# Pooled attention and a two-layer block: a second level of the seven-product scheme in the last two units of the first layer, with copies and sums moved to GpSimd

## The chip, the cores and the metric

The kernel runs on one core of one Trainium2 chip. The metric is device time in microseconds (us) of a whole execution; lower is better. In the profile the engines are called PE (TensorE, with PEld for its weight loads), DVE (VectorE), ACT (ScalarE), POOL (GpSimd) and SP (SyncE, which issues most of the DMAs).

## The reference, cut to what matters

All data are fp32: 8 batches, 8 heads, 576 positions, head size 64.

```python
k_p, v_p = mean of k and of v over groups of 8 positions      # 72 keys
attn = softmax(q @ k_p.T / 8) @ v_p                           # per batch and head
x = attn as (4608 tokens, 512)
h = x @ w_in                                                  # w_in: 512 x 2048
g = h + sin(alpha * h) ** 2 / (alpha + 1e-9)                  # alpha: per column of h
out = g @ w_out                                               # w_out: 2048 x 512
```

## The kernel before

**Both layers by seven products.** Each layer is a product of matrices cut in 2 x 2 blocks, done with seven block products in place of eight (the scheme of Strassen and Winograd). The price are sums of blocks on both sides: sums of w_in (`self.A[1..7]`), of x (`self.bt`, by `sums_of_x`, L817), and sums of the products afterwards. In the output layer the scheme is applied twice, one level inside the other, 49 block products for 64; the sums of w_out for that are made once (`load_w_out`, L725, and `inner_w`, L743).

**First layer.** `hidden(u, extra)` handles a unit of 512 tokens; there are nine units, 0 to 8. A unit has four groups J = 0 to 3, and a group has seven slots k = 0 to 6, so 28 slots, slot = 7 J + k. In a slot PE does one product p of the group, in the order 1, 5, 6, 2, 7, 3, 4. A product is four matmuls with 128 weights rows and columns and 256 tokens (L849). The profile holds two records for each such fp32 matmul. The products accumulate in four PSUM banks b1, b5, b6, b7 of a group; ACT copies one bank into the next where the scheme wants a product in two sums (L823) and makes the sine (L1009) and its square (L1016); DVE makes the sums h (L822) and g (L1061: one form with a PSUM input, 512 wide, and one with two SBUF inputs, 1024 wide). Then g goes to DRAM (`store_g`).

In the order of a unit, product 4 of group J waits until DVE has read the bank b7 in the L822 of slot 5 of that group. Where J = 1 the second half of product 4 may be put into slot 7.

**Second level in units 1 to 6.** Three of the 28 products of these units are done by seven small products in turn: product 5 in groups J = 2 and 3 (called i5), product 1 in J = 3 (i1). Such a product is seven matmuls of 128 tokens (L1039) in place of four of 256. `inner_product` cuts it into steps that `hidden` places between other products:

- a: products 1 and 5 into a spare bank y; ACT copies the first into half of the bank (L1043), the second into a small tile `m5` (L1045)
- b: products 6 and 2; ACT copies a quarter of the bank (L1049)
- d: product 7; DVE adds `m5` (L1054)
- e: products 3 and 4, which accumulate on what DVE wrote

The sums of w_in that these products need are made once, in unit 0 (`inner_w_in`), the sums of x in each unit (`inner_x`); both by `sums` on POOL (L807). In units 1 to 6 POOL also pools k and v (L132) and scales the softmax (L375), for the attention of the next batch that runs beside the first layer. i1 of the next group begins in slot 5 of the group before.

**The last two units.** There is no attention left to compute in units 7 and 8, and all their products are of the first level. `run` puts work for the output layer into their slots: in unit 7 w_out is loaded (`load_w_out`, four DMAs of 1 MB on SP into tiles `raw`), and a generator is advanced by `next(w)` in chosen slots: ACT copies the raw blocks into place (L716, 16 copies of 128 x 512), DVE makes the outer sums (L725, 16) and in unit 8 the inner sums of five of the seven weights (L743, four each; a sixth, p = 5, in slots 23 to 27; the seventh in the output layer). In slots 22, 25 and 27 of unit 8 the output layer starts (`outputs`): in slot 22 DVE makes four sums of 128 x 768 (L1303), in slots 25 and 27 PE does the first output products (L1364).

Each engine runs its own instructions in the order in which the program lists them, and waits in front of an instruction for what it needs; the slots are that order, written out by hand.

Of the kernel before, what the change touches and what calls it, by code (L numbers as in the profile page):

```python
# [40 lines left out]
class Kernel:  # L41
# [650 lines left out]
    def load_w_out(self, wp):  # L692
# [18 lines left out]
        def put(i, k):  # L711

            for j, t in enumerate(((b11, b12), (b21, b22))[i]):
                yield
                for n in range(2):
                    nc.scalar.copy(out=t[:, k:k + 4, n * P:(n + 1) * P].rearrange("p k (a c) -> p k a c", a=4),  # L716
                                   in_=raw[i, k][:, :, j, :, n, :])
        yield from put(0, 0)
        yield from put(1, 0)
        for c in range(0, kk, 2):  # L720
            if c == 2:
                yield from put(0, 4)
            yield
            s = slice(c, c + 2)
            tt = lambda o, x, y: nc.vector.tensor_tensor(out=o[:, s], in0=x[:, s], in1=y[:, s], op=OP.subtract)  # L725
            tt(t1, b12, b11)
            tt(t2, b22, t1)
            tt(b12, b22, b12)

            tt(t4, b21, t2)  # L730
            if c == 2:
                yield from put(1, 4)
        for p in (1, 2, 4, 6, 7):
            yield
            self.inner_w(p, wp)
        yield

    def inner_w(self, p, wp):

        nc = self.nc  # L740
        x = self.wb[p]
        b = lambda i, j: x[:, :, i - 1, j - 1, :].rearrange("p (k j) d -> p k j d", k=2)
        tt = lambda o, x, y: nc.vector.tensor_tensor(out=o, in0=x, in1=y, op=OP.subtract)  # L743
# [12 lines left out]
        return steps  # L756
# [24 lines left out]

    def inner_w_in(self):

        w = self.q_tile(0)[:]
        at = 0
        for p, J0 in ((5, 2), (1, 3)):
            n = self.NJ - J0
            A = self.A[p][:].rearrange("p k (J j m) -> p k J j m", j=2, m=P)[:, :, J0:]
            L = lambda i, j: A[:, j, :, i]
            s1, s2, s3, s4 = (w[:, at + i * n * P:at + (i + 1) * n * P].rearrange("p (J m) -> p J m", m=P) for i in range(4))  # L790
            at += 4 * n * P
# [3 lines left out]
    def inner_x(self, u):  # L795

        for p, x, out in ((5, self.bt[u][:, 0], self.last[:, 0:4 * P]),
                          (1, self.xT[u][:, 0:2, 0:TH], self.ex[:, 5].rearrange("p h x -> p (h x)")[:, 0:4 * P])):
            R = lambda i, j: x[:, i, j * P:(j + 1) * P]
            t1, t2, t3, t4 = (out[:, i * P:(i + 1) * P] for i in range(4))  # L800
            self.sums(((t1, R(0, 1), R(0, 0), OP.subtract), (t2, R(1, 1), t1, OP.subtract), (t3, R(1, 1), R(0, 1), OP.subtract), (t4, R(1, 0), t2, OP.subtract)))
            self.X2[p] = {1: R(0, 0), 2: R(1, 0), 3: R(1, 1), 4: t4, 5: t1, 6: t2, 7: t3}

    def sums(self, steps):
# [14 lines left out]
    def hidden(self, u, extra):  # L819
# [4 lines left out]
        sin, square, early = self.sin, self.square, lambda G: G.J == (0 if G.u else 1)  # L824
        two = 0 < u < self.B - 1
        split = lambda J: u == 0 and J == 2
        end = lambda J: u == 0 and J == 3

        def begin(J):
# [4 lines left out]
                                p5=None, i1=None, i5=None, early=J == (0 if u else 1))  # L834
            if two and J > 1:
                G.i5 = self.inner_product(G, 5, b5, 7)
            if two and J == 3:
                G.i1 = self.inner_product(G, 1, b1, 6)
# [21 lines left out]
        for slot in range(7 * self.NJ):  # L860
# [61 lines left out]
            elif k == 3:  # L922
                late = J == 0 and two
# [3 lines left out]
                if G.i1:  # L927
                    square(Q, 1, 1)
                    squares(Q, 0)
# [18 lines left out]
            elif k == 4:  # L948
                if G.i1:
                    copy(G.b7[:], G.b6[:])  # L950
# [16 lines left out]
            elif k == 5:  # L967
# [5 lines left out]
                N = None  # L973
                if two and J + 1 == 3:
                    N = self.next = begin(J + 1)
# [5 lines left out]
            else:  # L981
                if J == 0 and two and Q:
                    self.store_g(Q)
# [4 lines left out]
                if not N:  # L988
                    last()
                    extras()  # L990
                    product(G, 4, G.b7, part=(0, 1))
                    if not (two and J == 1):
                        product(G, 4, G.b7, part=(2, 3))
# [33 lines left out]
    def inner_product(self, G, p, ps, y):  # L1027
# [13 lines left out]
        def a():  # L1041
            products((1, 5), (y[:, 0], y[:, 1]), True)
            nc.scalar.copy(out=f[:, 0], in_=y[:, 0:1].to_broadcast([P, 2, P]))  # L1043
            m5[p] = self.sm.tile([P, 1, P], F32, name=f"m{p}", bufs=1)
            nc.scalar.copy(out=m5[p][:], in_=y[:, 1:2])  # L1045

# [4 lines left out]
        def d():  # L1051
            products((7,), (c[2],))
            x = ps.rearrange("p i t -> p (i t)")[:, P:3 * P].rearrange("p (i t) -> p i t", i=2)
            nc.vector.tensor_tensor(out=f[:, :, 1], in0=x, in1=m5[p][:].to_broadcast([P, 2, P]), op=OP.add)  # L1054

# [127 lines left out]
    def carry(self, u):  # L1183
# [6 lines left out]
        if u == 0:  # L1190
# [39 lines left out]
            at(9, self.load_q, 2)  # L1230
            at(23, self.inner_w_in)
            for e in range(2):
# [336 lines left out]
    def run(self):  # L1569
        nc, tc = self.nc, self.tc  # L1570
        pool = lambda s, n, b, **kw: s.enter_context(tc.tile_pool(name=n, bufs=b, **kw))
        with ExitStack() as top:
# [9 lines left out]
            with ExitStack() as one:  # L1582
# [35 lines left out]
                self.W2, self.X2 = {}, {}  # L1618
                self.R = {}
                self.first_batch()  # L1620
                self.s = self.hp.tile([P, 2, JW, 2, TH], F32, name="s", bufs=1)
                for u in range(self.NU):
                    x = self.carry(u)
                    if u == self.B - 1:
# [4 lines left out]
                        next(w)  # L1629
                        for i in (9, 10, 12, 13, 15, 16, 17, 18, 20, 21, 23):  # L1630
                            x[i].append(lambda: next(w))
                    elif u > self.B - 1:
                        homes.close()
                        homes = rest_homes
                        self.gq = pool(top, "gq", 1, side="right")
                        for i in (6, 10, 13, 14, 17, 20):
                            x[i].append(lambda: next(w))
                        x[5].append(lambda: self.load_g(0, ("r11", "r12")))
                        for i, f in zip((23, 25, 25, 27), self.inner_w(5, None)):
                            x[i].append(f)  # L1640
                        o = self.outputs()
# [48 lines left out]
```

## Time and profile before

| | |
|---|---|
| median of 3 runs | 900.12 us (899.48 to 900.14) |
| the profiled execution | 900.87 us, span 899.1 us |
| PE busy | 893.3 us, 99% of the span |
| DVE, ACT, POOL busy | 674.5, 440.9, 211.8 us |
| granted TensorE clock | 1.000 |
| unit 5, J = 2 to its slot 25 | 332.98 to 352.46 us |
| units 7 and 8 | about 416 to 515.7 us |
| POOL after 405 us | idle |

The span runs from the first to the last instruction of one execution under the profiler; its own time is 1.8 us longer, and the median of the runs is 0.75 us below that. Times in the views of the trace are us from the span's start; in a line of the timeline the first number is the start, the second how long the group of instructions lasts, and `x2` how many there are. A line of the chain has start, length, engine, tile written and line. In the groups of instructions, the numbers after the bar are the busy us in all and the mean ns of one.

### The profile page before, as it was taken

The page shows a single profiled execution, that of the slowest core. Times are in us where ns is not written, and L with a number is a line of the kernel's source. Part 1 is how long each engine was busy: PE and PEld are TensorE (multiplying, and loading weights), DVE is VectorE, ACT ScalarE, POOL GpSimd, SP SyncE. Part 2 cuts the span into 40 slices and gives each one's busy share as a digit, 9 for nine tenths or more (in the row PEclk, how much of TensorE's full clock was granted, in tenths as well). Part 3 has the DMA queues.
Part 4 walks back from the last instruction along what each step waited for, and adds up shares of the span by engine and source line. Part 5 has one row for each costly group of instructions (what it writes and reads, how often), then busy time and mean ns, then how long its engine had stood idle before and what let it go on. Part 6 is the DMA issues. An engine that isn't in the chain of part 4 may idle for free.

```text
span 899.1 us, 16074 instructions
## 1 busy us (share of the span) xinstructions
PE 893.3 (99%) x6226; PEld 814.7 (91%) x6226; DVE 674.5 (75%) x910; ACT 440.9 (49%) x1017; POOL 211.8 (24%) x217
## 2 busy tenths in 40 slices
PE   9999999999999999999999999999999999999998
PEld 5787888888888888888888999999999999999998
DVE  6786766768577685764557889898887896996885
ACT  5696776877768778687976621111121211111111
POOL 5798552824428253430000000000000000000000
PEclk9999999999999999999999999999999999999999
DMA  9946957759587595648216253716435345164002
GB/s 259 252 153 201 240 149 204 195 156 256 144 209 191 172 242 138 182 126 313 80 65 233 95 186 91 243 36 211 124 88 162 102 150 164 38 185 149 19 19 53
DMA packets 119531, 141.01 MB, mean 157 GB/s; under 512 B 45776, under 2 KB 86496, under 8 KB 119456
## 3 DMA queue, kind: packets, MB, share of 16 engines
q1 hardware_dynamic: 116288, 137.39, 52.8%
q10 hardware_dynamic: 3168, 2.61, 1.0%
q8 instruction: 49, 0.80, 0.4%
q14 instruction: 26, 0.21, 0.1%
HBM read 75.37 MB, written 47.19 MB: 136 GB/s over the span
## 4 chain that ended last, share of the span: by engine, by line
PE 98%; DMA 1%; POOL 0%; DVE 0%; issue 0%; ACTq 0%; ACT 0%; POOLq 0%
PE PS L849 46%; PE PS L1364 43%; PE PS L1039 3%; PE PS L318 2%; PE PS L613 2%; PE PS L626 1%; DMA p<-in_v_dram 1%; DMA q<-in_q_dram 0%; PE PS L571 0%; PE PS L290 0%; PE PS L279 0%; PE PS L479 0%; PE PS L569 0%; POOL tr L451 0%; PE PS L487 0%; POOL p L184 0%
## 5 line engine op out<-in xcount | busy, mean ns | idle before, releaser
L849 PE MATMUL PS<-home,a 128*128 128x256 f32 x1104 | 258.1, 381 | 0.1
L849 PEld LDWEIGHTS PS<-home,a 128*128 128x128 f32 x1104 | 205.3, 190 | 32.4 <-issue 4.5
L849 PE MATMUL PS<-home,as 128*128 128x256 f32 x768 | 182.7, 381 | 0.0
L849 PEld LDWEIGHTS PS<-home,as 128*128 128x128 f32 x768 | 141.7, 190 | 19.9 <-ACT PS L823 1.2
L1364 PE MATMUL PS<-s,wb 128*128 128x192 f32 x672 | 116.2, 326 | 0.0
L1016 ACT ACTIVATE s<-s,c 128x256 f32<-128x256 f32 (+1 forms) x228 | 113.5, 564 | 0.0
L1364 PEld LDWEIGHTS PS<-s,wb 128*128 128x128 f32 x672 | 110.4, 190 | 0.1
L822 DVE TENSOR_TENSOR h<-PS,p 128x512 f32<-128x512 f32 x72 | 49.3, 684 | 62.3 <-PE PS L849 36.9
L132 POOL TENSOR_TENSOR kvin<-kvin 96x768 f32<-96x768 f32 (+3 forms) x42 | 74.0, 1762 | 70.6 <-DMA kvin<-in_v_dram 69.0
L1009 ACT ACTIVATE s<-h,al 128x256 f32<-128x256 f32 x144 | 65.6, 509 | 38.5 <-DVE h L822 35.0
L1535 ACT COPY PS<-PS 128x192 f32<-128x192 f32 x42 | 12.7, 303 | 145.2 <-PE PS L1364 133.4
L1364 PE MATMUL PS<-r,wb 128*128 128x192 f32 x432 | 79.0, 326 | 0.0
L1364 PEld LDWEIGHTS PS<-r,wb 128*128 128x128 f32 x432 | 71.7, 190 | 0.1
L1364 PE MATMUL PS<-s,a 128*128 128x192 f32 x384 | 70.2, 326 | 0.0
L1009 ACT ACTIVATE s<-PS,al 128x256 f32<-128x256 f32 x144 | 60.1, 470 | 19.1 <-PE PS L849 18.1
L1061 DVE TENSOR_TENSOR h<-PS,s 128x512 f32<-128x512 f32 x36 | 24.8, 688 | 56.6 <-ACT s L1016 56.6
L1364 PEld LDWEIGHTS PS<-s,a 128*128 128x128 f32 x384 | 63.7, 190 | 0.0
L823 ACT COPY PS<-PS 128x512 f32<-128x512 f32 x72 | 41.4, 576 | 34.9 <-PE PS L849 30.1
L1061 DVE TENSOR_TENSOR h<-h,s 128x1024 f32<-128x1024 f32 x36 | 57.1, 1586 | 1.1 <-ACT s L1016 0.9
L1564 ACT COPY PS<-PS 128x192 f32<-128x192 f32 x42 | 12.7, 303 | 89.8 <-PE PS L1364 89.8
L1303 DVE TENSOR_TENSOR s<-r 128x768 f32<-128x768 f32 x54 | 51.4, 952 | 5.1 <-PE PS L1364 2.8
L1364 PE MATMUL PS<-s,we 128*128 128x192 f32 x288 | 52.7, 326 | 0.0
(218 smaller groups left out, 1316.7 us busy)
## 6 DMA issues: line engine op xcount, KB each, us to landing
g_bridge<-h SPq DMA_DIRECT2D x72, 512.0 KB
r<-g_bridge SPq DMA_DIRECT2D x15, 1536.0 KB
x<-g_bridge SPq DMA_DIRECT2D x8, 1536.0 KB
out_dram<-o SPq DMA_DIRECT2D x90, 96.0 KB
kvin<-in_k_dram SPq DMA_DIRECT2D x14, 576.0 KB
q<-in_q_dram SPq DMA_DIRECT2D x7, 1024.0 KB
kvin<-in_v_dram SPq DMA_DIRECT2D x14, 512.0 KB
aM<-tr SPq DMA_DIRECT2D x54, 92.0 KB
```

The lines of the kernel that those rows point to most:

```text
L132: self.nc.gpsimd.tensor_tensor(out=t[..., 0:w] if w > D else out, in0=t[..., 0:w], in1=t[..., w:2 * w], op=OP.add)
L318: nc.tensor.matmul(ps[e][r0 + r:r0 + r + q.shape[-1], h, :], q[s], kb[s, hp, :], start=True, stop=True)
L613: nc.tensor.matmul(o[r:r + 64], w, x, start=start and i < 2, stop=False, skip_group_check=True)
L822: add = lambda o, x, y: nc.vector.tensor_tensor(out=o, in0=x, in1=y, op=OP.add)
L823: copy = lambda o, x: nc.scalar.copy(out=o, in_=x)
L849: nc.tensor.matmul(ps[:, jj, :], self.A[p][:, kk, f * P:(f + 1) * P], x[:, kk, :], start=(start and n == 0), stop=(kk == 1), skip_group_ch ...
L1009: self.nc.scalar.activation(out=G.s[:, i, jj, j, :], in_=src[:, jj], func=AF.Sin, scale=self.al[:, f:f + 1])
L1016: self.nc.scalar.activation(out=x, in_=x, func=AF.Square, scale=self.c[:, f:f + 1])
L1039: nc.tensor.matmul(o, W[m][:, G.J - J0], X[m], start=start and n == 0, stop=True, skip_group_check=True)
L1061: add = lambda o, x, y: self.nc.vector.tensor_tensor(out=o, in0=x, in1=y, op=OP.add)
L1303: tt = lambda o, x, y, op: nc.vector.tensor_tensor(out=o, in0=x, in1=y, op=op)
L1364: nc.tensor.matmul(out, W[:, J // 2, J % 2, :], A[:, J, :], start=(start and J == 0), stop=(J == self.NJ - 1), skip_group_check=True)
```

## The change

- Units 7 and 8 take the second level for five products each: i5 in J = 1, 2, 3 and i1 in J = 2, 3. In units 1 to 6 nothing is changed (`busy` marks them, in place of `two`).
- The sums of w_in and x for that get homes of their own. In unit 7 (`homes_in_seven`): a free x tile and the two tiles `we1`, `we2` of w_out's inner sums. In unit 8 (`homes_in_eight`): tiles of the output layer's sums (`s30`, `s01`, `s20`) for x and for i5 of J = 1, and, from slot 8 on, the J = 0 slices of A[4], A[5], A[6], A[7] for the rest. All on POOL, in slots 0, 2 and 8.
- The 16 copies of w_out's raw blocks go from ACT to POOL, in two steps (slots 2 and 4 of unit 7) that stand in POOL's queue behind the sums for i5 and i1. DVE's 16 outer sums are now one to a step, in slots 15 to 25 of unit 7 and 1 and 2 of unit 8.
- The inner sums of w_out for p = 1, 2, 6, 7, 5 go from DVE to POOL (four instructions of 512 each); p = 4 stays on DVE in slot 9 of unit 8. In POOL's queue of unit 8 the order is: sums for i5 and i1 (8 of 128, then 4 of 128, then 8 of 256), weights p = 1, 2, 6, 7, 5.
- In the groups with i1 of units 7 and 8 the copy of b6 into b7 is made in slot 3 and not in slot 4.

Counted in the built programs, PE has 40 matmuls of 256 columns less and 70 of 128 columns more, POOL 72 instructions more. In unit 8, group J = 3, DVE's queue has the L822 of the group before, the L1054 of i1, the last L822, then the four L1303 of slot 22, then the L1054 of i5 (slot 23).

```diff
         def put(i, k):
             for j, t in enumerate(((b11, b12), (b21, b22))[i]):
+                for n in range(2):
+                    nc.gpsimd.tensor_copy(out=t[:, k:k + 4, n * P:(n + 1) * P].rearrange("p k (a c) -> p k a c", a=4),
+                                   in_=raw[i, k][:, :, j, :, n, :])
...
+        for k in (0, 4):
+            yield
+            put(0, k)
+            put(1, k)
+        for c in range(0, kk, 2):
+            s = slice(c, c + 2)
+            for o, x, y in ((t1, b12, b11), (t2, b22, t1), (b12, b22, b12), (t4, b21, t2)):
+                yield
+                nc.vector.tensor_tensor(out=o[:, s], in0=x[:, s], in1=y[:, s], op=OP.subtract)
-        for p in (1, 2, 4, 6, 7):
+        for p in (1, 4, 2, 6, 7, 5):
             yield
-            self.inner_w(p, wp)
+            self.inner_w(p, wp, None if p == 4 else nc.gpsimd)
...
+    def homes_in_seven(self, wo, x):
+        X = self.home(0, [P, 2048])
+        self.set_homes(X[:, 0:512], X[:, 512:1024], X[:, 1024:1152], X[:, 1152:1280])
+        we = [wo.tile([P, 3, 2, 2, P], F32, name=n)[:].rearrange("p a b c d -> p (a b c d)") for n in ('we2', 'we1')]
...
+        x[0].append(lambda: self.inner_x(7, (5,)))
+        x[0].append(lambda: self.inner_w_in(((5, 1, 4),), homes[:4]))
+        x[0].append(lambda: self.inner_x(7, (1,)))
+        x[0].append(lambda: self.inner_w_in(((1, 2, 4),), homes[4:]))
...
+    def homes_in_eight(self, x):
+        a, b = (self.gq.tile([P, self.NJ, self.T], F32, name=n)[:].rearrange("p J c -> p (J c)") for n in ("s30", "s01"))
+        self.set_homes(b[:, 0:512], a[:, 0:512], b[:, 512:640], b[:, 640:768])
+        used = [self.A[p][:, k, 0:JW * P] for p in (4, 5, 6, 7) for k in range(2)]
+        c = self.gq.tile([P, self.NJ, self.T], F32, name="s20")[:].rearrange("p J c -> p (J c)")
+        x[0].append(lambda: self.inner_x(8, (5,)))
+        x[0].append(lambda: self.inner_w_in(((5, 1, 2),), [c[:, i * P:i * P + P] for i in range(4)]))
+        x[2].append(lambda: self.inner_x(8, (1,)))
+        x[8].append(lambda: self.inner_w_in(((5, 2, 4), (1, 2, 4)), used))
...
-        two = 0 < u < self.B - 1
+        busy = 0 < u < self.B - 1
+        I5, I1 = ((2, 3), (3,)) if busy else {7: ((1, 2, 3), (2, 3)), 8: ((1, 2, 3), (2, 3))}.get(u, ((), ()))
...
-                        for i in (9, 10, 12, 13, 15, 16, 17, 18, 20, 21, 23):
+                        self.homes_in_seven(wo, x)
+                        for i in (2, 4, 15, 15, 16, 16, 17, 17, 18, 22, 22, 23, 23, 24, 24, 25):
                             x[i].append(lambda: next(w))
...
-                        for i in (6, 10, 13, 14, 17, 20):
+                        self.homes_in_eight(x)
+                        for i in (1, 2, 9, 9, 10, 27, 27, 27):
                             x[i].append(lambda: next(w))
                         x[5].append(lambda: self.load_g(0, ("r11", "r12")))
-                        for i, f in zip((23, 25, 25, 27), self.inner_w(5, None)):
-                            x[i].append(f)
```

More of the change, by code (lines that the diff above doesn't have):

```diff
@@ L713, in put, with inner_w @@
             for j, t in enumerate(((b11, b12), (b21, b22))[i]):
-                yield
[L715 to L722, printed above, removed]
-            yield
[L724 to L732, printed above, removed]
-        for p in (1, 2, 4, 6, 7):
-            yield
-            self.inner_w(p, wp)
+                for n in range(2):
[8 more added lines that the diff above has]
+            for o, x, y in ((t1, b12, b11), (t2, b22, t1), (b12, b22, b12), (t4, b21, t2)):
+                yield
+                nc.vector.tensor_tensor(out=o[:, s], in0=x[:, s], in1=y[:, s], op=OP.subtract)
+        for p in (1, 4, 2, 6, 7, 5):
+            yield
+            self.inner_w(p, wp, None if p == 4 else nc.gpsimd)
         yield
-    def inner_w(self, p, wp):
+    def inner_w(self, p, wp, eng=None):
         nc = self.nc
@@ L780, in abank, with inner_w_in @@
         return self.psum(shape, 5 + self.aturn)
[L782 to L788, printed above, removed]
+    def inner_w_in(self, groups, homes):
+        homes = iter(homes)
+        for p, J0, J1 in groups:
+            n = J1 - J0
+            A = self.A[p][:].rearrange("p k (J j m) -> p k J j m", j=2, m=P)[:, :, J0:J1]
@@ L922, in hidden @@
             elif k == 3:
-                late = J == 0 and two
+                late = J == 0 and busy
                 if Q and not late and not G.i5 and not split(J):
@@ L927, in hidden @@
                 if G.i1:
+                    if not busy:
+                        copy(G.b7[:], G.b6[:])
                     square(Q, 1, 1)
@@ L948, in hidden @@
             elif k == 4:
-                if G.i1:
+                if G.i1 and busy:
                     copy(G.b7[:], G.b6[:])
@@ L973, in hidden @@
                 N = None
-                if two and J + 1 == 3:
+                if J + 1 in I1:
                     N = self.next = begin(J + 1)
@@ L981, in hidden @@
             else:
-                if J == 0 and two and Q:
+                if J == 0 and busy and Q:
                     self.store_g(Q)
@@ L991, in hidden @@
                     product(G, 4, G.b7, part=(0, 1))
-                    if not (two and J == 1):
+                    if J + 1 not in I5 or J + 1 in I1:
                         product(G, 4, G.b7, part=(2, 3))
```

37 lines of the change are left out of this document (24 added, 13 removed).

## The prediction

> **What bounds the kernel now.** I read the chain that ended last first, from the page and then in order of time around the last three units of the first layer.
>
> ```profile
> PE 98%; DMA 1%; POOL 0%; DVE 0%; issue 0%; ACTq 0%; ACT 0%; POOLq 0%
> ```
>
> ```profile
> 332.98 0.44 PE PS L1039 x4
> ...
> 352.46 2.33 PE PS L613 x40
> ...
> 410.99 96.89 PE PS L849 x448
> 507.88 1.30 PE PS L1364 x8
> ```
>
> The second column is us. From 410.99 PE runs 448 records (224 matmuls, two records each) of the first layer in 96.89 us: 0.4325 us for one of 256 columns, 1.730 for a product of four, and not one gap. So PE's own time sets the end, a saved PE us is a won us, and a new PE wait is a lost one. The first two lines price the form that the change spreads: from 332.98 to 352.46, 19.48 us, unit 5 runs three second-level products (21 matmuls of 128 columns) among 34 of 256 columns. 34 × 0.4325 = 14.70, so 21 take 4.78: 0.2275 each, small waits included; four records without waits take 0.44, 0.22 each.
>
> Next, the timeline of the vector engines, because the change gives GpSimd (POOL) 72 instructions where it has had none.
>
> ```profile
> 67.27 1.26 POOL L688 TENSOR_TENSOR a<-a,a 128x512 f32<-128x512 f32 x1
> 67.51 2.11 DVE L1061 TENSOR_TENSOR h<-h,s 128x1024 f32<-128x1024 f32 x1
> 68.50 2.25 POOL L688 TENSOR_TENSOR as<-a,as 128x512 f32<-128x512 f32 x1
> ```
>
> A DVE instruction with two SBUF inputs, 1.21 when alone (507.22 in the same view), took 2.11: it ended 1.09 after the POOL instruction did. The POOL instruction behind it ended 1.13 after DVE, for 1.27 alone. They take turns whole. DVE instructions with a PSUM input are not touched: L822 and L1054 last 0.68 and 0.43 with POOL busy or idle. How a run of them alternates is seen at the start of unit 6:
>
> ```profile
> 362.96 0.94 DVE L817 TENSOR_TENSOR home<-home 128x512 f32<-128x512 f32 x1
> 363.43 0.78 POOL L807 TENSOR_TENSOR last<-home,last 128x128 f32<-128x128 f32 x1
> 363.82 0.94 DVE L817 TENSOR_TENSOR home<-home,home 128x512 f32<-128x512 f32 x1
> 364.18 0.90 POOL L807 TENSOR_TENSOR last<-home 128x128 f32<-128x128 f32 x1
> ```
>
> **What the change is worth on PE.** Ten products of 1.730 us go (17.30). Seventy matmuls of 128 columns come: 70 × 0.2275 = 15.9, or 15.4 at 0.22 without waits. Gain 1.4 us at the pace of units 1 to 6, 1.9 at best. I take 1.4, because the same hand-overs (PE, ACT copy, PE, DVE sum, PE) come with it. What follows is whether PE meets a new wait.
>
> **ACT.** 16 copies (L716, 0.6 each) leave unit 7; each second-level product adds 0.36 + 0.28 + 0.25 (L1043, L1045, L1049). In group J=2, which now runs both kinds and leads to another such group, I stacked ACT's queue from starts of unit 5 (0.40 or 0.36 per sine, 0.40 per square, 0.48 per copy of 512): it reaches the next L1043 7.3 us after i5.b starts, and PE asks for that copy at 7.7. Nothing lost; without this cover some tenths.
>
> **POOL's times.** Two inputs of 512 take 1.27 (L688 below), with the wait on the one before about 1.29; of 256, 0.73; of 128, 0.45. No row shows a copy. From below, a memset, which only writes, costs 0.85 ns per element (1071 less 422 over 768), 0.53 us for 512; from above, the sum's 1.27. I take 0.65, near the memset, since one stream in and one out is nearer to it than two in.
>
> ```profile
> L688 POOL TENSOR_TENSOR a<-a,a 128x512 f32<-128x512 f32 x4 | 5.1, 1272 | 0.0
> L807 POOL TENSOR_TENSOR q<-as 128x256 f32<-128x256 f32 x2 | 1.5, 728 | 0.0
> L1114 POOL MEMSET tr<- 128x1152 f32 x1 | 1.1, 1071 | 0.0
> L1601 POOL MEMSET ex<- 128x384 f32 x1 | 0.4, 422 | 0.0
> ```
>
> The Trainium skill, "GPSIMD Engine Reference", § 3.1, gives about 1.03 cycles per element at 1.2 GHz to bodies of up to two operations, an estimate of 0.44 us for 512 before dispatch; by it the copies would end some 2 us sooner, and the sum would be the same.
>
> **Unit 7.** It starts at 416.2; x sums for p5 run 417.2 to 420.3 (as in unit 6, against L817), weights for p5 (4 × 1.0) with one L1061 in between to 425.6, x and weights for p1 to 430.4. PE wants the first at slot 7, 427.5, and needs only what was ready by 421.5; it wants p1's at 436.8. Then 16 copies: 430.4 + 10.4 + 1.2 for one L1061 = 442. DVE's first L725 (slot 15) comes at 441 and needs only the first four. So they are nearly past each other: nothing lost. The w_out loads keep their place on SP; DMA moves their 4 MB by 427, before the copies. Cover: the spread slots 15 to 25. L1061 in J=1 waits for a copy at most, and unit 5 shows that such a wait (2.41 at 341.65, L822 behind it done at 344.67) still let PE start product 4 at 344.83.
>
> **Unit 8.** It starts at 463.9 (464.6 less 0.7). x sums and the first weights are done by 472; slot 7 is at 475.2. The sums in slot 8 wait for the J=0 slices of A[4], read last at 475.2 + 0.44 + 1.73 + 0.87 = 478.2. From there POOL never rests: 8 × 0.73, then inner_w of 1, 2, 6 and 7, 16 × 1.29, and two L1061 that hold it 1.2 each: 478.2 + 5.8 + 20.6 + 2.4 = 507, and inner_w(5) is still to come. J=2's own sums are there in time: the fifth (for i1.a, slot 12 at 484.5) at 482.
>
> Now J=3. Call T the start of its i5.b: 475.2 + 14.8 + 11.75 = 501.7. In DVE's queue the four L1303 of slot 22 (first sums of the output layer, two SBUF inputs) stand ahead of the L1054 of i5.d. In the kernel before they took 3.7 us and nobody waited:
>
> ```profile
> 503.02 0.95 DVE L1303 TENSOR_TENSOR s<-r 128x768 f32<-128x768 f32 x1
> 504.01 0.96 DVE L1303 TENSOR_TENSOR s<-s,r 128x768 f32<-128x768 f32 x1
> 504.88 0.95 DVE L1303 TENSOR_TENSOR s<-r 128x768 f32<-128x768 f32 x1
> 505.75 0.95 DVE L1303 TENSOR_TENSOR s<-r,s 128x768 f32<-128x768 f32 x1
> ```
>
> In unit 5, where T is 347.68, DVE is free at T − 1.0 and PE starts i5.e, which needs that L1054, at T + 4.17:
>
> ```profile
> 346.03 0.68 DVE L822 TENSOR_TENSOR h<-PS,s 128x512 f32<-128x512 f32 x1
> ...
> 347.68 0.39 PE L1039 MATMUL PS<-last,q 128*128 128x128 f32 x2
> ...
> 351.85 0.39 PE L1039 MATMUL PS<-home,q 128*128 128x128 f32 x2
> ```
>
> Without POOL the four end at T + 2.7 and L1054 at T + 3.2: covered by 1.0 us. With POOL saturated they take turns: −1.0, a first wait of 0.55 (0 to 1.13), 0.95 + 3 × 0.82 of DVE (0.95 less the 0.13 that a waiting instruction saves), 3 × 1.13 of POOL: T + 6.35, L1054 done at T + 6.8. PE waits 2.6 us (2.1 to 3.2). Behind i5.e stand the first output matmuls, products 7, 3 and 4; PE has no gap later in which to make this up, so all of it reaches the end.
>
> **Other parts.** 20 sums (L743) leave DVE for POOL, ten L1054 come: DVE is lighter and not the bound. The last POOL sum delays one L1303 of slot 27 by up to 1.1 us; its product comes 5 us later. inner_w(5) is ready by about 513; it is used 45 us into the output layer. Nothing for either.
>
> **Sum.** −1.4 + 2.6 = +1.2 us. The profiled execution took 900.87, 899.1 of it span; it should become 902.1 (span 900.3). The median of the runs, 900.12, lies 0.75 below it, so I predict 901.3, about +0.13%. A measurement of this kernel tells some 0.2% (1.8 us) from no change.
>
> **Rivals.**
> Hidden (0.22): the turns do not cost what I say, and the gain shows. For it: once two DVE instructions went past a waiting POOL one undisturbed (31.30 and 31.90, 0.67 and 0.68, POOL 2.09 for 0.59). If DVE passes in pairs, one turn of 1.13 is left and the wait is 0.3 or less. Against it: six unit starts show strict turns. 900.12 − 1.4 = 898.7; at the best pace 898.2, just over 0.2% (0.07 of the 0.22). The Trainium skill, "SBUF — State Buffer", § Who interferes with whom, lets whichever starts first keep the shared ports for its whole instruction; by that rule and the rows at 67.27 I keep this rival small.
>
> Slow copies (0.12): a POOL copy costs what a sum does. Then 16 × 1.29 reach past 451, and in J=2 of unit 7 eight two-input DVE instructions (seven L725, one L1061) each wait a turn of 1.13 before the L822 that product 4 waits for: 9 us, less the time that DVE idles there and 0.9 of slack, about 4.3 at PE. 901.3 + 4.3 = 905.6. It decides from some 1.0 us a copy on. Against it: the memset's slope.
>
> Small waits (0.08): hand-overs in four groups with both kinds, without the attention's matmuls between them, lose 0.3 us each: 902.5.
>
> **Numbers.** My case has 0.58; its wait of 2.1 to 3.2 and gain of 1.4 to 1.9 give 900.3 to 902.3, with the tail of the DVE queue behind unknown; I put 0.22 of it above 901.9. Slower: 0.22 + 0.12 + 0.08 = 0.42. Faster: 0.07. Same: 0.36 + 0.15 = 0.51. The range from 898.5 to 903.6 leaves out most of the slow copies and the best pace.
>
> **Right or wrong.** Right: in unit 8, J=3, the four L1303 last about 2 us each with POOL instructions between them, PE stands 2 to 3 us before i5.e, waiting for L1054, and nowhere else in units 7 and 8 for more than some tenths. Wrong: L1303 at 0.95 (hidden), POOL copies above 1.0 with waits at product 4 in J=2 of unit 7 (slow copies), waits for ACT at i1.b (small waits), or POOL idle before 500.

## The result and the profile after

The changed kernel is slower by about half a per cent: a median of 904.35 us (five runs, 903.14 to 905.12) against 899.48 us (five runs of the kernel before, 898.73 to 900.14); the ratio of the times is 1.0048, 95% interval 1.0036 to 1.0060 (the medians alone would give 1.0054). The profiled execution took 905.12 us, 903.3 of it span. The prediction said 901.3, 898.5 to 903.6: the sign is right, the size is far too small.

In what follows line numbers are those of the changed kernel: L873 is the matmul of 256 columns (L849 before), L1065 that of 128 (L1039), L1390 the output layer's (L1364), L1080 the sum into PSUM that i5.e waits for (L1054), L845 the sums h (L822), L1087 the sums g (L1061), L1329 the output layer's sums (L1303), L736 the inner sums of w_out (L743), L715 the copies (L716). In kernels with lines added the numbers move by one to three.

The chain that ended last, as in the first fence of before: PE's share has gone from 98% to 41%, because the chain now leaves PE and runs back through a load.

```profile
PE 41%; DVE 1%; DMA 1%; issue 0%; SPq 0%; DVEq 0%
```

The timeline of PE where unit 8 ends. The number in brackets is the idle time ahead of the line, with what ended it: PE finishes product 2 of the last group and waits for L1080.

```profile
504.68 1.89 PE L873 MATMUL PS<-home,a 128*128 128x256 f32 x8
509.42 0.49 PE L1065 MATMUL PS<-home,as 128*128 128x128 f32 x2 [2.85 <-DVE PS L1080]
```

The timelines of DVE and POOL at the same place show why L1080 is late. Before, the four sums of slot 22 lasted 0.95 each. Now each takes its turn with a POOL sum, and the L1080 of i5 stands behind all four:

```profile
501.19 2.01 DVE L1329 TENSOR_TENSOR s<-r 128x768 f32<-128x768 f32 x1
503.23 1.91 DVE L1329 TENSOR_TENSOR s<-s,r 128x768 f32<-128x768 f32 x1
505.07 2.02 DVE L1329 TENSOR_TENSOR s<-r 128x768 f32<-128x768 f32 x1
507.01 2.01 DVE L1329 TENSOR_TENSOR s<-r,s 128x768 f32<-128x768 f32 x1
508.95 0.42 DVE L1080 TENSOR_TENSOR PS<-PS,s 128x256 f32<-128x256 f32 x1
...
502.46 1.87 POOL L736 TENSOR_TENSOR a<-wb,a 128x512 f32<-128x512 f32 x1
504.30 1.98 POOL L736 TENSOR_TENSOR wb<-wb 128x512 f32<-128x512 f32 x1
506.23 1.98 POOL L736 TENSOR_TENSOR as<-wb,a 128x512 f32<-128x512 f32 x1
```

So far this is what the prediction described. The table of stretches shows what it did not have. Its columns are the stretch, its length, busy us and instructions of PE, PEld, DVE, ACT and POOL, then the granted TensorE clock, DMA share and GB/s:

```profile
507.00:509.00 2.00, 0.00 (x0) 0.00 (x0) 2.00 (x3) 0.64 (x2) 2.00 (x2) 1.00 0.00 0
509.00:510.60 1.60, 1.18 (x8) 1.18 (x9) 1.60 (x4) 0.43 (x1) 1.52 (x2) 1.00 0.00 0
510.60:512.00 1.40, 1.40 (x7) 1.40 (x6) 0.64 (x1) 0.89 (x3) 1.40 (x1) 0.50 0.00 0
512.00:514.00 2.00, 2.00 (x6) 1.56 (x5) 0.00 (x0) 1.28 (x3) 1.59 (x2) 0.50 0.94 351
514.00:516.00 2.00, 2.00 (x11) 1.74 (x10) 0.69 (x1) 0.34 (x1) 0.00 (x0) 0.99 0.47 173
```

From 510.6 to 514.0 the clock is 0.5. PE is busy all that time and does half as much: records of 256 columns start 0.43 us apart instead of 0.216. The drop begins 1.2 us after PE has started again, so PE is not idle in it, and a table of busy times alone would not show it. It costs 3.4 / 2 = 1.7 us.

The chain in order of time then passes through the load that the output layer waits for. The last piece is the first matmul of a product that began at 535.00 without a wait before; it now waits 0.2 us:

```profile
519.74 8.38 DMA r<-g_bridge
...
535.75 3.37 DVE x L1329
...
539.16 5.96 PE PS L1390 x35
```

POOL itself does what was forecast. The groups of its copies: the first eight (`wb<-wb`) last 0.61 us each; in the mean of the second eight (`wb<-r`) one that waited for DVE is included.

```profile
L715 POOL COPY wb<-r 128x512 f32<-128x512 f32 x8 | 5.5, 736 | 0.0
L715 POOL COPY wb<-wb 128x512 f32<-128x512 f32 x8 | 4.5, 613 | 0.0
```

### The profile page after: what moved, and what is told of

The parts are those of the page before. It is cut to its first block, busy times and chain, and to the rows that moved or that the text cites. A ratio compares the mean times of both kernels' runs of the same rounds, so it can differ in the third digit from the quotient of the medians.

```text
span 903.3 us, 16343 instructions
## 1 busy us (share of the span) xinstructions
PE 893.0 (99%) x6286; PEld 815.4 (90%) x6286; DVE 671.3 (74%) x900; ACT 440.5 (49%) x1039; POOL 277.4 (31%) x289
## 5 line engine op out<-in xcount | busy, mean ns | idle before, releaser
L873 PE MATMUL PS<-home,a 128*128 128x256 f32 x1072 | 254.7, 382 | 0.1
L873 PEld LDWEIGHTS PS<-home,a 128*128 128x128 f32 x1072 | 198.9, 191 | 30.9 <-issue 4.6
L873 PE MATMUL PS<-home,as 128*128 128x256 f32 x720 | 174.2, 382 | 0.0
L873 PEld LDWEIGHTS PS<-home,as 128*128 128x128 f32 x720 | 131.1, 190 | 17.9 <-ACT PS L846 1.6
L1390 PE MATMUL PS<-s,wb 128*128 128x192 f32 x672 | 116.2, 326 | 0.0
L1042 ACT ACTIVATE s<-s,c 128x256 f32<-128x256 f32 (+1 forms) x236 | 115.5, 556 | 0.0
L1390 PEld LDWEIGHTS PS<-s,wb 128*128 128x128 f32 x672 | 110.4, 190 | 0.1
L845 DVE TENSOR_TENSOR h<-PS,p 128x512 f32<-128x512 f32 x72 | 49.2, 683 | 63.3 <-PE PS L873 40.1
L1390 PE MATMUL PS<-r,wb 128*128 128x192 f32 x432 | 79.7, 328 | 0.0
L1390 PEld LDWEIGHTS PS<-r,wb 128*128 128x128 f32 x432 | 72.1, 191 | 0.0
L1390 PE MATMUL PS<-s,a 128*128 128x192 f32 x384 | 70.2, 326 | 0.0
L1390 PEld LDWEIGHTS PS<-s,a 128*128 128x128 f32 x384 | 63.7, 190 | 0.0
L1087 DVE TENSOR_TENSOR h<-PS,s 128x512 f32<-128x512 f32 x36 | 24.7, 686 | 46.9 <-ACT s L1042 46.9
L1329 DVE TENSOR_TENSOR s<-r 128x768 f32<-128x768 f32 x54 | 53.6, 992 | 5.5 <-PE PS L1390 2.8
L1087 DVE TENSOR_TENSOR h<-h,s 128x1024 f32<-128x1024 f32 x36 | 55.3, 1537 | 2.5 <-ACT s L1042 2.3
L1390 PE MATMUL PS<-s,we 128*128 128x192 f32 x288 | 52.7, 326 | 0.0
```

The source lines that it names most:

```text
L845: add = lambda o, x, y: nc.vector.tensor_tensor(out=o, in0=x, in1=y, op=OP.add)
L873: nc.tensor.matmul(ps[:, jj, :], self.A[p][:, kk, f * P:(f + 1) * P], x[:, kk, :], start=(start and n == 0), stop=(kk == 1), skip_group_ch ...
L1042: self.nc.scalar.activation(out=x, in_=x, func=AF.Square, scale=self.c[:, f:f + 1])
L1087: add = lambda o, x, y: self.nc.vector.tensor_tensor(out=o, in0=x, in1=y, op=OP.add)
L1329: tt = lambda o, x, y, op: nc.vector.tensor_tensor(out=o, in0=x, in1=y, op=op)
L1390: nc.tensor.matmul(out, W[:, J // 2, J % 2, :], A[:, J, :], start=(start and J == 0), stop=(J == self.NJ - 1), skip_group_check=True)
```

## A measure that leaves the start out

Profiled executions do not reach one and the same instruction of the first layer at the same time: the 321st record of PE starts at 33.84 us in before, at 34.05 in after, and between 32.05 and 33.62 in the ten kernels below, all with the same instructions up to there. That is 2 us of scatter ahead of this record, while the first loads come in, and more than the change was to be worth; what makes it was not tested. So beside the times I compare one stage: from PE's 3201st record (in unit 6, the same instruction in all kernels) to its 2000th record from the end (in the output layer, also the same). From that one to the last record it is 324.84 us in every kernel.

| kernel | stage, us | against before | ratio of the times (95%) |
|---|---|---|---|
| before | 189.98 | | |
| after | 194.14 | +4.16 | 1.0048 (1.0036 to 1.0060) |
| e1_hold | 189.19 | −0.79 | 0.9994 (0.9985 to 1.0003) |
| e2_busy | 193.47 | +3.49 | 1.0029 (1.0020 to 1.0038) |
| e3_three | 190.26 | +0.28 | 1.0007 (0.9998 to 1.0016) |
| e5_pool_alone | 190.00 | +0.02 | 1.0003 (0.9994 to 1.0011) |
| e6_spaced | 189.75 | −0.23 | 0.9989 (0.9980 to 0.9998) |
| e7_five | 197.18 | +7.20 | 1.0072 (1.0056 to 1.0087) |
| e8_six | 193.36 | +3.38 | 1.0036 (1.0022 to 1.0049) |
| e9_pool_spaced | 190.01 | +0.03 | 0.9999 (0.9990 to 1.0007) |
| e10_twice | 189.38 | −0.60 | 0.9992 (0.9983 to 1.0001) |
| e11_three | 193.83 | +3.85 | 1.0051 (1.0036 to 1.0065) |

The stage is of one execution each, the ratio of four to eleven runs. The stages of e2, e7 and e8 contain 1.1 us that PE waits in unit 7 and that has nothing to do with their edits (see e6). Where two kernels differ by less than 0.1%, the intervals do not tell them apart.

## Experiments

Theory: the change wins about 1.5 us on PE, and loses it to one wait, at i5.e of the last group of unit 8, which POOL's inner sums make by taking turns with DVE; the wait costs its own length and after that a stretch at half clock. Rivals: the new products themselves or POOL's copies lose the time, with the wait an accident beside it; or the clock falls for another reason than PE's idle time.

**e1_hold: take away what POOL does during the four sums.** One small POOL sum reads the result of the fourth L1329, and POOL's sums for p = 7 and 5 stand behind it; those for p = 6 move from slot 27 to slot 20, ahead of it.

```diff
+        nc.gpsimd.tensor_tensor(out=self.held[:], in0=A[0, 0][3][:, 0, 0:64], in1=A[0, 0][3][:, 0, 64:128], op=OP.add)
...
-                        for i in (1, 2, 9, 9, 10, 27, 27, 27):
+                        for i in (1, 2, 9, 9, 10, 20, 27, 27):
```

> GpSimd's eight sums for p = 7 and 5 stand behind a small GpSimd sum that reads the result of the last of the four L1329 of slot 22; nothing else is changed against the changed kernel. Turns theory (the L1329 take turns with GpSimd, the L1080 behind them comes late, PE idles, and the idle costs a stretch at half clock): the four L1329 last 0.95 us each, PE does not wait before i5.e of J = 3 in unit 8, the granted clock stays at 1.0, and the time falls by 3.0 + 1.7 us from the changed kernel, to 1.0 to 1.5 us under the kernel before (ratio 0.9985). Hand-over theory (the second level itself makes PE wait in these units, GpSimd or not): L1080 is still late, the wait of about 3 us stays, ratio 1.004 to 1.005.

Measured: 899.23 us against 899.61, ratio 0.9994 (0.9985 to 1.0003). The timelines of DVE, POOL and PE:

```profile
500.18 0.95 DVE L1329 TENSOR_TENSOR s<-r 128x768 f32<-128x768 f32 x1
...
502.91 0.95 DVE L1329 TENSOR_TENSOR s<-r,s 128x768 f32<-128x768 f32 x1
503.78 0.42 DVE L1080 TENSOR_TENSOR PS<-PS,s 128x256 f32<-128x256 f32 x1
...
503.94 0.32 POOL L1514 TENSOR_TENSOR held<-s 128x64 f32<-128x64 f32 x1 [3.79 <-DVE s L1329]
...
505.40 0.38 PE L1065 MATMUL PS<-home,as 128*128 128x128 f32 x2
```

With POOL held for 3.79 us the four sums take 0.95 again, L1080 is ready 1.2 us before PE wants it, no wait stands ahead of i5.e and the clock is 1.0 after it. The time fell short of what was expected: 0.9994 in place of 0.9985, and the stage is 0.79 us under before where 1.0 to 1.5 were expected; most of what is missing is in the gain, below. Setting the two kernels' PE records side by side, after lies 1.02 us behind e1 ahead of the wait (the start), 4.01 behind at i5.e, 5.80 at 514.03 and 5.95 from 539.16 on: 3.0 us for the wait, 1.8 from there to the end of the slow stretch, 0.15 at the load. So 4.8 of the 4.95 us lost against e1 are in this one place.

**e2_busy: the same wait, but PE not idle in it.** Thirteen matmuls whose result nobody reads stand ahead of i5.e.

```diff
                     product(G, 2, G.b1)
+                    if u == 8 and J == 3:
+                        for _ in range(13):
+                            nc.tensor.matmul(self.psum([P, 4, P], 6), self.full[:], self.full[:].unsqueeze(1).to_broadcast([P, 4, P]), start=True, stop=True)
                     G.i5.e()
```

> The changed kernel with 13 matmuls of ones (bf16, 512 columns, some 0.2 us each) put in front of i5.e of J = 3 in unit 8, into a bank that nobody reads then: PE waits as long, but works meanwhile. If the half clock after the wait comes from PE's idle time: no stretch at 0.5, L1080 at the same place, and 1.7 us less than the changed kernel (ratio to before 1.003 in place of 1.005). If the slow matmuls after the wait come from something else that happens there (GpSimd at work, the banks, the DMAs): they stay at double length, and the ratio stays at 1.005.

Measured: 902.18 us, ratio 1.0029 (1.0020 to 1.0038). The timeline of PE, and the stretch in which after was at half clock:

```profile
506.91 2.97 PE L960 MATMUL PS<-full 128*128 128x512 bf16 x13
509.94 0.49 PE L1068 MATMUL PS<-home,as 128*128 128x128 f32 x2
```

```profile
510.60:512.00 1.40, 1.40 (x10) 1.38 (x9) 1.15 (x1) 1.31 (x4) 1.32 (x2) 1.00 0.00 0
512.00:514.00 2.00, 2.00 (x11) 1.76 (x10) 0.23 (x1) 1.27 (x4) 2.00 (x2) 1.00 0.68 252
```

DVE's sums are as slow as in after, i5.e comes as late, yet the clock stays at 1.00. So it is PE's idle time that brings on the half clock. Its price by the medians is 0.0019 of the time, 1.7 us; the two intervals touch, so the size rests on the traces: 3.41 us at half clock in after, and stages that lie 1.8 us apart once 1.1 us is taken off e2's. That 1.1 us is a wait in unit 7 that after's profile does not have; e6 and e10 are about it. What is left above before is the wait. Nor does the half clock stand in one execution alone: 3.4 us of it lower the mean clock by 0.0019, and the mean clock of the five runs of after is 0.997 to 0.999, that of the eleven runs of e2 0.999 to 1.000.

**e3_three: one turn less.** Three of the four sums stay in slot 22, the fourth goes to slot 24, behind L1080.

```diff
-        for _ in inner(0, 0):
-            pass
+        first = inner(0, 0)
+        for _ in range(2):
+            next(first)
+        yield
+        for _ in first:
+            pass
...
-                        for i in (22, 25, 27):
+                        for i in (22, 24, 25, 27):
```

> Only three of the four L1329 stay in slot 22; the fourth goes to slot 24, behind the L1080 of i5. Turns theory: one turn of 1.95 us less in front of L1080, so PE waits 0.9 to 1.1 us in place of 2.85 before i5.e, no half clock, and the time is 0.3 to 0.8 us under the kernel before (ratio 0.9995). If the half clock came with any wait: 1.7 us more, ratio 1.001 to 1.0015. Hand-over theory: the same 1.004 to 1.005.

Measured: 899.91 us, ratio 1.0007 (0.9998 to 1.0016). The timeline of PE:

```profile
506.11 0.49 PE L1065 MATMUL PS<-home,as 128*128 128x128 f32 x2 [0.91 <-DVE PS L1080]
```

The wait falls from 2.85 to 0.91, by 1.94 us, one turn; and the clock stays at 1.0. One turn less saves the turn and the slow stretch together: 3.9 us of the stage, 0.3 of it at the load. The time did not come out as expected: 1.0007 in place of 0.9995, its runs 3.0 us apart. The stage explains its own +0.28: the wait is 1.18 us from start to start, and with 0.07 at the load it eats up a gain of 0.97 (see the gain, below).

**e5_pool_alone: GpSimd's part without the second level.** Copies and inner sums on POOL as in after, units 7 and 8 with products of the first level only.

```diff
-        I5, I1 = ((2, 3), (3,)) if busy else {7: ((1, 2, 3), (2, 3)), 8: ((1, 2, 3), (2, 3))}.get(u, ((), ()))
+        I5, I1 = ((2, 3), (3,)) if busy else ((), ())
```

> The GpSimd part alone: copies and five weights' sums on GpSimd as in the changed kernel, but units 7 and 8 run all products at the first level and make no sums for a second level. Turns theory: GpSimd reaches its sums earlier and no L1080 stands behind the L1329, so PE does not wait: the time of the kernel before, ratio 0.9997 to 1.0005. If GpSimd's copies or sums cost PE time in another place (late weights, late sums of w_out): ratio over 1.001.

Measured: 899.82 us, ratio 1.0003 (0.9994 to 1.0011); the stage is 190.00 against 189.98. So the move to POOL shows no cost by itself. It costs where a second-level product waits behind the sums that it slows.

**e6_spaced and e9_pool_spaced: copies that leave a gap.** In e2 the timelines of POOL, DVE and PE in unit 7 had shown this:

```profile
433.71 4.51 POOL L715 COPY wb<-r 128x512 f32<-128x512 f32 x8
...
434.90 4.39 DVE L1090 TENSOR_TENSOR h<-h,s 128x1024 f32<-128x1024 f32 x1
...
439.95 0.70 PE L873 MATMUL PS<-home,a 128*128 128x256 f32 x2 [0.86 <-DVE h L845]
```

The same DVE sum in after, at the same distance from the start of the copies:

```profile
435.53 1.59 DVE L1087 TENSOR_TENSOR h<-h,s 128x1024 f32<-128x1024 f32 x1
```

In after it came in behind one copy; in e2 it got in only behind six copies, the last of the row among them, and product 4 of group J = 1 of unit 7 waited. The profiles of e7 and e8 below are like e2 (4.38 us), those of after, e1, e3 and e11 like after. e6 is e1 with a small POOL sum behind each copy that reads the copy's result, so that a copy can't follow a copy at once; e9 is e5 with the same.

```diff
                     nc.gpsimd.tensor_copy(out=t[:, k:k + 4, n * P:(n + 1) * P].rearrange("p k (a c) -> p k a c", a=4),
                                    in_=raw[i, k][:, :, j, :, n, :])
+                    nc.gpsimd.tensor_tensor(out=self.held[:], in0=t[:, k + 3, n * P:n * P + 64], in1=t[:, k + 3, n * P + 64:(n + 1) * P], op=OP.add)
```

> The kernel of e1 (GpSimd's 512-wide sums for p=7 and 5 held until the four VectorE sums of slot 22 are done), and behind each of GpSimd's sixteen copies of the second layer's weights a small sum of GpSimd over 64 columns that reads the copy's result: no copy can then start in the same instant in which the one before ends. The profile of e2 showed what the copies can do otherwise: seven of them in a row kept one VectorE sum of 128x1024 in unit 7 from ending for 4.39 us (1.6 us in the profiles of after and e1), and TensorE waited 1.02 us for it. If such executions are what kept e1 at 0.9994 and spread its runs over 2.5 us, the runs fall to about 898.3 us (ratio 0.9985) with less than 2 us between fastest and slowest, the VectorE sum takes at most 1.7 us, and TensorE waits nowhere in unit 7 for more than some tenths. If e1's shortfall has another cause (a smaller gain on TensorE, the start of the kernel), this one comes out as e1 did: 0.9994, 899.2 us.

> The kernel of e5 (GpSimd copies and sums the second layer's weights, no second level in units 7 and 8), with the same small sum behind each copy as in e6. TensorE has the work of before. If the copies cost time in some executions, this one is at 1.0000 with a narrower spread than e5's 2.6 us; if e5's 1.0003 and its spread have another cause, nothing changes against e5. Should the small sums themselves get in the way of VectorE, it is slower than e5, by up to 1 us.

Measured: e6 899.02 us against 900.09, ratio 0.9989 (0.9980 to 0.9998), its runs 2.0 us apart (2.5 in e1). e9 899.76, ratio 0.9999 (0.9990 to 1.0007), its runs 1.5 us apart (2.6 in e5). The sum in e6:

```profile
433.95 1.22 DVE L1088 TENSOR_TENSOR h<-h,s 128x1024 f32<-128x1024 f32 x1
```

It starts and ends undisturbed, and no gap of TensorE in unit 7 is over 0.11 us. The median moved the expected way, but the intervals of e1 and e6 overlap. That the row of copies shuts DVE out in some executions is shown by the traces; that this made e1's shortfall is not shown by the times. e6 is the one kernel whose interval lies wholly below before, by its upper end only just; its profiled stage gains only 0.23 us, because there the output layer's product waits 0.64 us for the load of r22.

**e7_five: a longer wait.** The fourth sum of slot 22 (128 x 768) is made twice.

```diff
+        a = A[0, 0]
+        tt(a[3], a[2], a[6], OP.subtract)
         yield
```

> The changed kernel with a fifth VectorE sum of 128x1024 in slot 22 (the fourth one done again, with the same result), ahead of the sum that product 5 of the last group of unit 8 needs. It takes one more turn with GpSimd, 1.95 us, so TensorE's wait grows from 2.85 to 4.8 us. What follows on the clock is in dispute. If the half clock after a long wait lasts for one stretch of fixed length (3.4 us in after), the time is after plus 1.95: 906.3 us, ratio 1.0075, with about 3.4 us at half clock. If its length goes with the wait, about 5.7 us at half clock, and 907.5 us, ratio 1.0088.

Measured: 906.41 us, ratio 1.0072 (1.0056 to 1.0087). The timeline of PE, and stretches with PE's busy time and the clock alone:

```profile
510.96 0.49 PE L1065 MATMUL PS<-home,as 128*128 128x128 f32 x2 [4.80 <-DVE PS L1080]
```

```profile
511.00:512.00 1.00, 1.00 (x6) 0.78 0.00 0
512.00:513.00 1.00, 1.00 (x4) 0.50 0.00 0
513.00:514.00 1.00, 1.00 (x4) 0.50 0.32 121
514.00:515.00 1.00, 1.00 (x4) 0.52 1.03 381
```

The wait is 4.80 as expected. Half clock from 511.56 (the first stretch's mean of 0.78) to 514.97 is 3.4 us, as long as after the wait of 2.85. The stretch does not grow with the wait. The mean clock of its four runs is 0.996 to 0.998.

**e8_six and e11_three: how much idle time is too much.** e2 with six and with three of the thirteen matmuls.

```diff
-                        for _ in range(13):
+                        for _ in range(6):      # e11_three: 3
```

> The kernel of e2 with six instead of thirteen matmuls of 128x512 of no use ahead of product 5: they keep TensorE busy for the first 1.3 us of the wait and leave it idle for about 1.55 us. VectorE's sums, and so the end of the wait, are as in after and e2. If the half clock comes only after an idle time between the 1 us of e3 and the 2.85 us of after and 1.55 us is short enough, the clock stays at 1.0 and the time is that of e2 (902.2 us, ratio 1.0029). If 1.55 us is already enough, some 3.4 us at half clock follow and it is 903.9 us, ratio 1.0048.

> The kernel of e2 with three matmuls of no use instead of thirteen: TensorE is idle for about 2.15 us ahead of product 5 of unit 8's last group, between the 1.51 us of e8 (clock 1.0 throughout) and the 2.85 us of after (half clock for 3.4 us). If 2.15 us bring on the half clock, the time is that of after, 904 us, ratio 1.0045 to 1.005; if not, that of e2 and e8, 902 to 903 us, ratio 1.003 to 1.0035.

Measured: e8 903.18 us, ratio 1.0036 (1.0022 to 1.0049); e11 904.32 us, ratio 1.0051 (1.0036 to 1.0065). PE's timeline and a stretch behind it, of e8:

```profile
509.50 0.49 PE L1068 MATMUL PS<-home,as 128*128 128x128 f32 x2 [1.56 <-DVE PS L1083]
```

```profile
511.00:513.00 2.00, 2.00 (x12) 1.00 0.40 146
```

and of e11:

```profile
507.97 0.49 PE L1068 MATMUL PS<-home,as 128*128 128x128 f32 x2 [2.22 <-DVE PS L1083]
```

```profile
509.00:510.00 1.00, 1.00 (x7) 0.67 0.00 0
510.00:512.00 2.00, 2.00 (x7) 0.50 0.67 249
512.00:513.00 1.00, 1.00 (x4) 0.63 0.99 377
```

1.56 us idle leave the clock alone, 2.22 bring on the half clock, again for 3.4 us (509.34 to 512.75). The line lies between, in these executions. It is the clock that decides this: the interval of e8's times holds both times that were expected. The six runs of e11 scatter from 902.43 to 906.23, more than any other kernel's, as they would if the same idle time set off the slow stretch in some executions only; but one of 905.30 had a mean clock of 1.0, so that alone does not explain them.

The clock's own records tell more of when the half clock comes. In all twelve profiles PE's first stretch at full clock begins between 4.2 and 9.2 us, and every later change of the clock comes a whole number of 3.4133 us after that: in after, e7 and e11 505.173 us later, which is 148 × 3.4133, and the half clock lasts one such period. So it does not begin a set time after the restart, but where a period ends. Divided so, the period ahead of the half clock holds 2.22 us of PE's idle time in after, 2.82 in e7 and 2.05 in e11; periods that hold 0.91 (e3), 1.53 (e8) and 1.99 (e7, the one before) are followed by full clock. The idle time behind the last matmul of the kernel fits: a period with 2.03 us of it (e6) is followed by half clock, one with 1.93 (e3) is not. What seems to count is thus the idle time inside one period, with the line near 2 us (the ends of matmuls are modelled in the profile, so the hundredths carry little), and a wait of 2.2 us that a period's end cuts in two may leave the clock alone. No profile here shows such a wait; it would fit the mean clocks of e11's runs, 0.997 to 1.000.

**e10_twice: a longer row of copies.** e1 with each of the last eight copies done twice.

```diff
+                    for _ in range(2 if k else 1):
-                    nc.gpsimd.tensor_copy(out=t[:, k:k + 4, n * P:(n + 1) * P].rearrange("p k (a c) -> p k a c", a=4),
+                        nc.gpsimd.tensor_copy(out=t[:, k:k + 4, n * P:(n + 1) * P].rearrange("p k (a c) -> p k a c", a=4),
...
```

> The kernel of e1 with each of the last eight of GpSimd's copies done twice (the same data to the same place): the row of copies from r lasts 9.0 instead of 4.5 us. In three profiles so far (e2, e7, e8) the VectorE sum of 128x1024 that starts in this row ended only with the row's last copy (4.38 us) and TensorE waited 1.02 us; in three others (after, e1, e3) it ended after 1.6 us. If in some executions the row keeps VectorE out until it ends, the sum takes about 8.9 us in those, TensorE waits about 5.5 us, and the eleven times fall into two groups, near 899.2 and near 903.7 us. If VectorE is let in at the latest after some 4.4 us, whatever the row, the slower group is as in e1, and the spread stays at 2.5 us around 899.2 us. If the wait in e2, e7 and e8 came from something else, nothing changes against e1.

Measured: 899.19 us against 899.55, ratio 0.9992 (0.9983 to 1.0001); its runs lie only 1.4 us apart. There is no second group near 903.7. The experiment was badly built: a copy to the place that the one before wrote waits for it, so copies inside a pair start 0.68 us apart, the first ended 0.06 earlier, while copies of different pairs still start 0.56 apart, before the other has ended. The row has the gaps of e6 in every second place, and the sum got in without any delay:

```profile
434.40 1.22 DVE L1088 TENSOR_TENSOR h<-h,s 128x1024 f32<-128x1024 f32 x1
```

It says nothing of how long an unbroken row would shut DVE out. It agrees with e6, in one profile each, that a row with such gaps did not hold the sum.

## Why the prediction was wrong

**The place, the mechanism and the wait: right.** The wait stands where it was put, made by the four sums in the way described (turns of 1.9 to 2.0 us), 2.85 us long where 2.6 (2.1 to 3.2) was forecast. e1 and e3 show the cause: without POOL's sums the wait is gone, with one turn less it is 1.94 shorter. "Nowhere else in units 7 and 8 for more than some tenths" holds in after's profile, and fails in those of e2, e7 and e8.

**The failed step: "Sum. −1.4 + 2.6 = +1.2 us".** It prices a PE wait at its own length. The sum lacks a term: after the wait PE runs 3.4 us at half clock, 1.7 us lost. It is not in the rivals either, so the range ended at 903.6. Removing PE's idleness alone (e2) took 1.7 us off; lengthening the wait (e7) left the term as it was. The trace of before has no long PE wait in this part and could not show the price. The Trainium skill does: "TensorE: Matmul & The Clock Gate", Part 1, says that a window of about 3.4 us of idleness puts the clock to half until a busy window has passed, and its section "Why this matters for your kernels" asks for no idle gaps above some 3 us. The length of the stretch agrees here (3.4 us); the idle time that sets it off is shorter (2.22 us were enough, 1.56 were not). By that page a forecast of 2.6 us, 3.2 at its upper bound, was near enough to its limit to make this a rival: +1.2 + 1.7 = +2.9 us.

**The gain was mis-sized too.** −1.4 was said to contain small waits. In e1, where the big wait is gone, the stage gains 0.79. PE's gaps of over 0.06 us between 405 and 560 us, counted from start to start, are 0.66 us more in e1 than in before: new are 0.06 twice and 0.17 to 0.18 twice at hand-overs of the new products (once each in unit 7 and unit 8), and 0.18 at the output layer's product that waits for the load of r22. Without these gaps it would gain 0.79 + 0.66 = 1.45 us. That is the 1.4 of the text, but the hand-overs were to be inside it: net of them it is 0.97. At the pace of their starts without any wait (0.432 and 0.222 us a matmul) the exchange is worth 40 × 0.432 − 70 × 0.222 = 1.74, so −1.4 left 0.34 for small waits; they are 0.77, the 0.48 at the hand-overs and 0.29 in waits of under 0.06 each. Another 0.18 goes to the load, whose chain the text had passed over.

**Summed anew, by the stage:** PE's gaps in after, added one by one from the starts of its records, are 0.47 at hand-overs, 3.11 at the wait (3.01 between two starts and 0.10 between the records of the matmul behind it), 1.68 in the slow stretch and 0.33 at the load, 5.59 together. The stage grew by 4.16, which leaves −1.43 for the work, as in e1. Against the forecast of +1.2 the stage's +4.16 has 0.4 less gain, 0.5 more wait, 1.7 of half clock and 0.3 at the load. The medians are 4.87 us apart; the ratio of 1.0048 stands for 4.3 us, its interval for 3.2 to 5.4.

**Starting point.** The forecast was reckoned from 900.12; the same kernel's later runs have medians from 899.5 to 900.1. Against the five runs of before that stand beside the result, 899.48, the forecast of +1.2 would have been 900.7: the higher start hid 0.6 us of the miss, by luck.

**The rivals.** "Hidden": refuted by the turns. "Slow copies": a copy costs 0.61, one each 0.56 in a row, near the 0.65 that was taken, so the rival's price did not apply; but a neighbour of it was there: not the length of a copy but the lack of a gap between copies holds up the L1087 of J = 1 in unit 7 ("waits for a copy at most" was wrong for e2, e7 and e8). ("Some 2 us sooner" for the lower estimate of a copy should have been 16 × 0.21 = 3.4 us; nothing else rests on it.) "Small waits": at 0.06 and 0.17, smaller than the 0.3 it wanted. POOL's times hold at the wait: the four L1329 were forecast as turns of about 1.95 and are 1.91 to 2.02. Its sums for p = 5 end at 518.0 and not by about 513, which PE does not feel.

## What to carry to other kernels

Price a wait of the bounding engine with what comes behind it: here a wait of TensorE of 3.1 us cost 4.8, one of 1.56 us only itself, so bringing a wait under some 1.5 us is worth more than the same microseconds elsewhere. When work moves to GpSimd, list every VectorE sum with two SBUF inputs that will run beside it and look at what is queued behind those; holding GpSimd back for 3.8 us at the one critical place gave back all of the loss, and made TensorE wait nowhere for the work that it delayed, which is wanted much later. A gain of 0.2% needs a measure that leaves out the scatter of the start, such as the time between two instructions that all versions share.

## What the runs showed of the hardware that was not expected

- The half clock begins after PE has restarted (1.2 us after in after, 0.6 in e7, 1.4 in e11), where a period of 3.4133 us counted from the first full clock ends; it lasts one such period whether PE had idled for 2.22, 2.85 or 4.80 us, and comes while PE is busy.
- GpSimd copies of 128 x 512 in a row start 0.56 us apart and last 0.61, so each starts before the one ahead has ended. A VectorE sum with two SBUF inputs that came 1.2 us into such a row of eight was let in behind one copy in four profiles (1.6 us) and only behind the whole row in three (4.38 us). Between the GpSimd sums beside the four L1329 it got its turn behind each one (1.9 to 2.0 us, in after, e2 and e3). In the rows of e6 and e10, where every second instruction of GpSimd began 0.06 to 0.08 us after the one ahead had ended, it was not held at all (1.22 us). Why a row without gaps holds it in some executions only stays open.
